# A new written order for all five engines from block 1 on in a fused attention and two-layer mixture kernel

## Chip, cores and metric

The kernel runs on one core of one Trainium2 chip. The metric is the device time of one execution in microseconds (us); the kernel before has three measured runs and one more that was profiled. All times below are of that profiled execution unless they are called a median.

## What is computed

Everything is float32, and the result has to have float32's accuracy.

```
out_up    = repeat4( softmax(scale * q_d k_d^T) v_d )      q_d, k_d, v_d: means over 4 positions
out_local = softmax(scale * q k^T where |i-j| < 4) v
x = heads_to_channels(out_up + out_local)                  q, k, v: 4 x 8 x 576 x 64 -> x: 2304 x 512
x = (sigmoid(x @ w_gate) * (x @ w_val)) @ w_out            512 -> 1536 -> 512
h = x @ w_in;  g = h * tanh(softplus(h));  out = g @ w_out2   512 -> 2048 -> 512
```

## The kernel before

**Tiling.** The four batches are four blocks of 576 tokens. A block has its attention and then the first layer; the second layer follows for all tokens at the end. Each wide product is split into a high and a low part and computed as three matmuls into one PSUM tile.

**The long products of a block.** `m1_half` (L1416 to L1418) multiplies a weight slice of the ring `R` with the tokens: 12 matmuls, 128x128 weights against 288 columns, into a tile `ps_m`. `m1` (L1442, L1443) makes the gate on ACT and DVE, and `fin` splits it into `G` (L425 on ACT, L426 on DVE). `m1out_part` (L1429, L1431, L1433) multiplies `G` with the output weights, 12 matmuls of the same shape into `ps_o`. `m1out` copies finished tiles to `stage` (L1473, L1476 on ACT), POOL makes differences of them (L1485), and `put` splits these (L1459 on ACT, L1460 on DVE) and parks them in DRAM (`x2d`, issued by SP at L1492 and L1498).

**Attention of the next block beside it.** While the long products of block b run, the attention of block b+1 runs in pieces between them. Its products are short ones. Two are full-height transposes or 72-row ones against an identity: L604 (loaded `tok` to `kT`, `qT`), L738 and L856. Four have operands of 64 rows or 64 columns: L699 (pooled scores), L753 (pooled values), L808 (local scores) and L896 (local values). The local softmax is L816 and L820 on DVE (mask and maximum, reading the PSUM tile of L808), L833 on ACT (exponential with row sums), L651, L652 and L844 on DVE (normalizing), L856 on PE, the copy L308 on ACT, L896 on PE and the join L915 on DVE. The copies out of L604 are L310 on ACT. Short products use a pool `at` of three PSUM banks, long products a pool `mm` of five.

**A stay** is from here on a run of short products on PE between two long ones.

**Loads and their queues.** SP issues the attention's loads (`tok` L552, `araw` L557, `vw` L572), the reload of the weights (`d<-wd`, L453, 512 KB each) and most stores. Weights that come in as 64-bit words are narrowed: POOL L390, then DVE L398, L399 and L403; the narrowed tiles are written to `wd` and read again. POOL issues the first loads of the second layer, `xu` (L1957, in `units2` and after it, 512 KB each).

**The second layer.** `product` (L2029 to L2031) is 12 matmuls of 256 columns, `m2out` (L2042 to L2044) is three of 512; `phase` puts them together. The first products follow two warm-up matmuls (L2013).

**What sets the order.** The steps of a block are traced in one way, which fixes the instructions and what each depends on. Then `written_order` rearranges every engine's instructions by a dictionary `RUNS`, one string for each of PE, ACT, DVE, POOL and SP. A word `step x n` moves the reading position by `step` and takes the next `n` instructions of the engine as traced:

```
step, _, n = word.partition("x")
at += int(step)
seq += own[at:at + int(n or 1)]
at += int(n or 1)
```

Each engine then has its instructions pinned in that order. It runs them one after another: where the next has to wait, all behind it on that engine wait too. The strings say nothing of times; each instruction starts when its operands are there.

Of the kernel before, what the change touches and what calls it, by code (L numbers as in the profile page):

```python
# [138 lines left out]
    'PE': '''0x1583 184x8 -192x12 204x4 -208x12 196x4 24x4 -228x24 204x4 -208x24 208x8 -216x16 12x12 -24x12 212x8  # L139
        24x2 2x2 2x2 -242x12 232x2 -234x24 198x2 -200x36 8x12 146x2 2x2 2x2 24x2 2x2 2x2 2x2 -194x12 8x24  # L140
        138x2 2x2 2x2 2x2 24 1 -2 -170x24 8x24 8x21 19x5 -24x3 83 -63x19 16x16 12x12 -24x8 16x36 8x24 -32x5
        1 29x12 -43 1 40x12 -28x4 24 1 1x12 -15 1 12x16 8x12 8x6 -14x4 -24 33 -34x7 16x4 24x8 -20x12 32
        -50x5 60 1 -2 1 -19x15 -40x12 80x2 2x2 2x2 -90x4 28x9 41x2 36x2 2x2 -40x2 4x2 -90x3 83x2 36x2 -36x2
        -52x8 -45x5 120x2 -82x4 -15x3 12x12 54x2 2x2 2x2 28x8 -34x2 -68x12 112x8 -64x12 -52x12 116x13 3x2
        2x2 -138x12 122x2 2x4 2x2 -17x3 10x2 2x2 -56x12 68x2 2x2 -106x12 96x2 -122x12 -32x12 52x12 68x2
        -12x2 -16x12 6x2 2x2 2x2 -40x12 28x24 36x4 -40x24 40x4 12x4 -14x2 2x2 -8x2 2x2 2x4 -56x12 72x2 2x2
        2x2 2x2 -12x2 36x2 2x2 2 -43x2 2x2 2x2 -72x12 86x2 2x2 1 2x2 -4x2 2x2 -80x24 -68x12 84x12 28x4
        -16x12 4x4 2x2 -64x2 64x2 -8x2 10x4 -12x2 2x4 -70x10 88x4 24x4 -56x12 44x4 24x4 -76x12 64x4 -64 87x4
        -91x11 80x4 24x4 -112x12 100x4 24x2 -122x12 110x2 -112x12 100x6 2x2 -4x2 2x2 24x2 2x2 -134x24 8x24
        80x2 2x2 -78x24 42x2 2x2 32 -31x2 -36x12 53x3 -30x2 -28x12 16x24 4x48 8 11x12 -23x11 -20x5 1 -2 1  # L150
        28x24 4x24 -56x4 24x2 26x12 -38 37x12 -49 48x4 4x12 -16x4 24x8 -20x12 32x13 3 1 -2 1 -7x3 -40x24
        68x4 2x2 2x2 -8x2 8x2 -8x2 -58x12 76x2 2x2 2x2 -38x2 38x2 -90x24 54x2 -56x12 46x2 2x2 2x2 24x4
        -68x24 44x4 24x8 -64x24 64x13 3x2 -5x3 2x4 2x2 2x2 -86x24 8x24 56x2 2x2 -30x24 -34x2 2x2 2x2 40x12
        -20x2 2x2 -12x2 2x2 20x12 -30x2 2x2 24x24 44x12 -56x24 60x12 -72x16 72x12 -84x4 12x6 2x2 -4x2 2x18
        80x12 -80x6 2x2 2x2 42x12 -28x2 -14x12 4x2 2x2 -8x2 2x2 4x2 -48x2 2x2 2x2 34x2 2x2 24x64 12x18 2x2 6
        11x12 -28x2 -8x2 2x2 2x2 -40x12 52x24 -47x11 36x600 36x12 -48x36 24x12 12x12 -24x12 -36x12 36x72
        24x24 -48x24 36x12 12x12 -24x12 -36x12 36x13 13x12 -24x12 -13 36x12 -24x12 48x12 -48x12 48x12 -60x12
        48x12 -36x12 -36x12 84x12 -48x24 27x2 -29x12 12x3 24x12 6x12 -52x13 3 -4x2 100x12 -110x2 15x3 135x12
        -132x3 -36x3 36x12 6x12 66x12 -78x3 42x12 -130 81x12 -39x3 -18x3 36x3 33x3 -96x3 150x12 6x12 -108x3
        132x12 -168x3 72x3 117x4 -217x3 33x3 90x2 61x12 -73 -78x3 160 -62x12 50x7 -72x3 -81x6 -9x3 36x6 30x3  # L160
        21x3 -24x3 78x12 -147x3 33x3 33x3 78x12 45x12 -51x12 66x12 -69x12 24x12 27x12 -189x3 21x3 -6x3 36x3
        132x12 -189x3 21x3 33x3 33x3 -60x3 -57x3 207x12 -132x3 21x3 -81x3 33x3 75x3 96x12 -75x3 -93x3 -6x3
        210x2 -176x3 33x2 61x12 65x9 -147 33x3 21x3 -84x3 117x12 38 -30x12 81x12 -222x3 33x3 -81x3 21x3 33x3
        30x3 21x3 -24x3 15x3 96x12 -30x12 102x12 -186x3 96x12 -75x3 96x12 9x12 -171x3 21x3 186x12 -30x12
        -186x3 33x3 -42x3 54x3 15x3 21x3 -78x3 33x3 33x3 -57x3 36x3 -6x3 33x3 21x3 33x3 33 5x12 6x12 -35x2
        -96x3 138x12 12x12 12x12 -165x3 33x3 21x3 -84x3 21x3 -24x3 33x3 18x3 12x3 18x6 12x3 105x12 -114x3
        21x3 51x12 -72x3 -24x3 126x12 -96x3 -24x3 24x3 15x3 81x12 -159x3 21x3 60x3 21x3 -72x2 25x3 -24x3
        21x3 21x3 -55 90x3 21x3 -69x3 93x12 -81x3 -57x3 114x3 15x3 -60x3 78x12 -147x3 21x3 21x3 21x3 54x3
        -54x3 -54x3 21x3 42x3 -24x3 3x12 21x3 15x3 15x3 -36x12 18x3 15x6 15x3 -6x3 -15x12 24x12 -66x12 24x15
        36x12 -48x3 18x12 -15x3 -6x3 33x12 3x12 6x12 33x12 -42x12 3x12 18x12 -123x3 27x3 15x3 75x12 -123x3  # L170
        27x3 111x12 -93x3 93x12 -78x2 -47x3 75x12 36x12 -108x3 27x2 -15 14 78x12 -78x3 12x3 15x3 48x12 -33x3
        -48x3 78x2 -5x2 -50x3 72x3 -21x12 9x9 -34 -4 -21x2 79x12 -90x3 57x12 -36x2 97x12 -30x12 -90x3 33x3
        -40 117x12 -57x3 33x3 21x3 -75x12 -39x3 -76 54x3 33x3 -72x3 150x12 -129x3 147x3 -96x3 -24x3 147x3
        -54x12 -108x3 111x12 -72x3 78x12 -114x3 117x12 -75x3 33x3 -93x3 171x12 -150x3 33x3 39x3 -96x3 33x3
        33x6 57x12 81x12 -126x12 159x12 -30x12 -168x3 75x12 -93x3 60x12 -51x3 33x3 75x12 -54x3 -81x3 21x3
        87x3 -96 62x12 -36x3 114x12 -93x3 -77x2 33x3 72x3 99x12 -30x12 -90x3 33x3 33x3 -132x3 111x12 -204x3
        33x3 33x3 21x3 54x3 33 56x12 -68x2 69x12 -30x3 30x12 15x3 -81x2 -95x3 204x3 -228x3 33x3 33x3 38
        -18x3 -45x3 33x3 84x12 60x12 -147x3 75x12 -60x3 90x3 -33x12 -15x3 57x12 3x12 -63x3 63x12 -132x3
        -18x3 147x12 -99x2 -5x3 9x3 -10 15x2 -8x3 9x3 -6x3 78x12 3x12 -109 33x3 -18x3 57x3 33x3 9x3 -36x3
        21x3 9x3 -84x3 57x3 9x3 -60x3 45x3 9x3 6x18 36x12 -48x2 46x2 -38x12 -22x3 19x5 -24x7 48x14 -45x7  # L180
        14x10 14x10''',
    'ACT': '''0x292 6 25 -28 -5 1 29 -18 20 -29 28 3 -31x2 -14 16 -7 -2 37 -2 -34x2 27 8 -30 -6 -17 16x2 3x2 -5 5
        -6 3 26 -24 5 -8 1 3 5 -8 4 5x2 -7 3 5 20 -64 52 22 -36 4 -4 -48 57 20 -29x4 27 -19 -41 -22 57x3 8
        -18 14 -12 6 9 -21 14 5 6 -17 5 -10 15 -9 -5 8 -4 7 7 -6 -2 7 -7x3 6 -5 1 -5 4 7x2 -8 10 -9x2 -4x2 9
        -4 8 -6 3 3 -12 -48 59 -2 -9 9x2 -18 17 -12 4 -5 15 -14 7 1 -2 2 5 2x2 -4 8 -43 27 2 25 -4 3 -29 29
        -9 -16x2 -5 4 15 3 -20 12 -13 1 7 -27 30 8 -5 6 -2 -2 -5 1 -20x2 16 5 -26 25 24 -67 41 -25 49 -11 1
        -42 39 2 -7 4 -5 5 10 -55 27 -28 42 -16 20 -6 -21 1 -5x2 22 3 3 -7 6 4 -2 -8 12 -2 -7 11 -5 -16 5 -2
        14 2 -13 6 -2 -6 13 -11 4x2 10 -24 38 -25 -2 9 -55 -7 53 2 11 -12 -55 73 -15x2 16 -4 -27 22 -70 65
        16 -35 4 12 -20 7 30 -33 3 37 -38 2 9x2 1 4 -84 95 -34 17 2 -19 12 -8 7 1 22 -19 -2 1 6 -93 90 2 12
        -21x2 8 -9x2 10 2 -2 -6 -98 62 30 20 -6x2 -4x2 -11 7 -3 6 -9 9 -2 2 9 3 -13 3 -6 2 6 4 -12 2 6 -7 -3  # L190
        12 3 -12 5 1 -10 4x2 12 -9 -2 20 -3 2 -9 -8 9 -8 4 -11 7 -3 -8 7 -10 2 19 -19 15 -5 -3 6 2 -69 62 -8
        10 5 -5x2 6 -3 -5 2 -3 6x2 11 -17 10 -7 8 -3 -11 10 1 3x2 -4x2 -13x2 27x2 -16 -14 -64 63x2 13 -3 2
        -3 3 2 -5 11 2 -14 3 -4 7 6 2 -9 14 -15 9 -18x2 8 -2 -12 14 10 -13 5 8 -12 11 -14 15 -13x2 13 -12 -2
        2x2 10 -9 11 6 -19 7 -6 10 -13 2 4 -5 2 11 2 -12 -2 3 11 -12 2 10 -13 2x2 -9 10 11 5 -11 -5 -4 1 2x2
        7 -17 11 -2 2x2 2 11x2 -6 -4 -7 4 -2 2 4 -2 -4 6x2 -14 13 -25 25x2 -11 7 13 -11 1 -4 12 -12 9 -8x2
        -3 2x4 5 1 -5 2 3 -7 4 -2 2x5 1 -2 11 -11 2 -3x2 9 -2 -8x2 19 -20 7 -8x2 8 -3 -7 18 -13 1 7 13 -21
        -2 1 -9 8 9 -4 -7 17 -12 3 1 -6 11 -7x2 20 -12 -25 10 3 21 -18 4 1 -7 6 -7 -20 27x2 -4 8 -13 6x2 16
        -43 20 12 -4 11 -9 -4x2 3 7 -8 -30 29 9 -14 24 -22 5 4 -38 32 5 10 -11 7 -8 -8 -22 28 -5 4x2 17 -8
        -40 34 4 -5 -8 18 -7 -13 18 -39 25 5x2 -4 -28 39 -10 9 -5 9 -5 -6x2 4x2 7 -2 -7 1x2 -8 -37 47 -36 35
        -6 5 -33 34 -2 -2 6 -32 26 -25 24x2 2 -3 5 -2 1x3 2 -25 22 -9 9 6 -17 14 -3 -4x2 2 2 -12 14 6 -17 5  # L200
        10 -8 -4x2 3x3 3 4 -2 -8 -5 7 10 -2 -5 -6x2 4x2 -4 10 -5 10 -15 14 -12 3 1 -6x2 9 -6 -3 7 9 -16x2 7
        -4x3 8 -8 17 -13 -6x3 7 -4 10 -16 4 10 -11 1 1x2 8 6 -16 -4 3 3 3 -4 9 -6 -5 4x2 3 -8 3 13 -8 -4 10
        -11 2 1 -5 4x2 -4 6 -4 7 -2 -4 5 -6 5 -6 5x2 -5''',
# [2073 lines left out]
```

## Time and profile before

| | us |
|---|---|
| median of three runs | 1012.32 |
| lowest, highest | 1008.45, 1016.48 |
| the profiled execution's own time | 1007.65 |
| its span in the profile | 1005.8 |

The span is what the profile's rows lie in, from 0 to 1005.8 us; 1.85 us of the execution's time lie around it. In the span, the attention of block 0 and what goes with it lasts to 185.7 us, the long products of the blocks to 613 us, and the second layer from there to the end. A matmul row's own duration includes its pipeline, so the distance from one start to the next is what it costs PE. The trace keeps two rows for one matmul of L808 and L896 and one row for a transpose and for a long matmul.

### The profile page before, as it was taken

How to read it: one execution, taken by the hardware profiler on the slowest of the kernel's cores; microseconds unless marked ns; L12 is line 12 of the kernel's file. 1: busy time of each engine (PE TensorE's matmuls, PEld its weight loads, DVE VectorE, ACT ScalarE, POOL GpSimd, SP SyncE). 2: the span in 40 equal slices, each digit the busy share in tenths (PEclk: the TensorE clock that was granted, in tenths of full speed). 3: DMA queues.
4: the chain of work that ended last, by engine and by line, in shares of the span. 5: the costliest groups of instructions: out<-in, count | busy, mean ns of one | idle time of the engine just before them, and what ended most of it. 6: DMA issues, size and time to landing. Idle time of an engine off the chain costs nothing.

```text
span 1005.8 us, 20645 instructions
## 1 busy us (share of the span) xinstructions
PE 977.7 (97%) x8113; PEld 911.0 (91%) x8113; DVE 673.9 (67%) x1097; ACT 560.9 (56%) x1259; POOL 251.8 (25%) x276
## 2 busy tenths in 40 slices
...
GB/s 225 156 235 185 186 253 262 238 137 163 178 118 180 214 92 165 102 151 116 234 199 126 87 170 228 331 192 252 183 249 265 282 231 240 124 147 140 154 56 105
DMA packets 160897, 184.86 MB, mean 184 GB/s; under 512 B 68512, under 2 KB 124064, under 8 KB 160288
## 3 DMA queue, kind: packets, MB, share of 16 engines
...
## 4 chain that ended last, share of the span: by engine, by line
PE 76%; DMA 10%; DVE 6%; ACT 3%; issue 2%; POOL 1%; SPq 1%; ACTq 0%; POOLq 0%; DVEq 0%
PE ps_m L1416 9%; PE ps_m L1417 9%; PE ps_m L1418 9%; PE po L2042 6%; PE po L2044 6%; PE po L2043 6%; PE h L2029 6%; PE h L2031 6%; PE h L2030 6%; PE ps_o L1429 3%; PE ps_o L1433 3%; PE ps_o L1431 3%; DMA tok<-in_q_dram 1%; DMA d<-wd 1%; DMA raw<-in_moe_w_out_dram 1%
## 5 line engine op out<-in xcount | busy, mean ns | idle before, releaser
L1416 PE MATMUL ps_m<-R 128*128 128x288 f32 (+2 forms) x768 | 232.4, 304 | 0.0
L1418 PE MATMUL ps_m<-R 128*128 128x288 f32 (+2 forms) x768 | 227.6, 296 | 0.0
L1417 PE MATMUL ps_m<-R 128*128 128x288 f32 (+2 forms) x768 | 227.6, 297 | 0.0
L2029 PE MATMUL h<-xu,R 128*128 128x256 f32 x512 | 145.0, 283 | 3.5 <-ACT hs L2175 2.1
L1416 PEld LDWEIGHTS ps_m<-R 128*128 128x128 f32 x768 | 144.6, 189 | 3.8 <-issue 1.3
L1418 PEld LDWEIGHTS ps_m<-R 128*128 128x128 f32 x768 | 144.9, 189 | 0.3 <-issue 0.2
L1417 PEld LDWEIGHTS ps_m<-R 128*128 128x128 f32 x768 | 144.9, 189 | 0.1
L2030 PE MATMUL h<-xu,R 128*128 128x256 f32 x512 | 144.4, 282 | 0.0
L2031 PE MATMUL h<-xu,R 128*128 128x256 f32 x512 | 144.0, 282 | 0.0
L1429 PE MATMUL ps_o<-G,R 128*128 128x288 f32 x384 | 115.3, 301 | 0.0
L2042 PE MATMUL po<-wo,g 128*128 128x512 f32 x288 | 113.0, 393 | 1.1 <-ACT o L2080 1.1
L1433 PE MATMUL ps_o<-G,R 128*128 128x288 f32 x384 | 113.3, 295 | 0.3 <-DVE R L426 0.3
L1431 PE MATMUL ps_o<-G,R 128*128 128x288 f32 x384 | 113.0, 294 | 0.0
L2043 PE MATMUL po<-wo,g 128*128 128x512 f32 x288 | 112.5, 391 | 0.0
L2044 PE MATMUL po<-wo,g 128*128 128x512 f32 x288 | 111.4, 392 | 0.0
L2029 PEld LDWEIGHTS h<-xu,R 128*128 128x128 f32 x512 | 97.1, 190 | 8.3 <-ACT hs L2175 2.7
L426 DVE TENSOR_TENSOR R<-d,R 128x512 fp32r<-128x512 f32 (+1 forms) x108 | 79.3, 744 | 33.2 <-ACT R L425 33.1
L2030 PEld LDWEIGHTS h<-xu,R 128*128 128x128 f32 x512 | 97.3, 190 | 3.4
L390 POOL TENSOR_SCALAR rebias<-raw 128x512 f32<-128x512 f32 x33 | 56.5, 1712 | 174.8 <-DVE d L403 73.3
L2031 PEld LDWEIGHTS h<-xu,R 128*128 128x128 f32 x512 | 97.1, 190 | 0.0
L425 ACT CAST R<-d 128x512 fp32r<-128x512 f32 (+1 forms) x108 | 67.3, 642 | 45.3 <-DMA d<-wd 23.5
L1429 PEld LDWEIGHTS ps_o<-G,R 128*128 128x128 f32 x384 | 71.9, 188 | 1.2
...
## 6 DMA issues: line engine op xcount, KB each, us to landing
d<-wd SPq DMA_DIRECT2D x54, 512.0 KB
xu<-x2d SPq DMA_DIRECT2D x45, 512.0 KB
raw<-in_moe_w_out_dram SPq DMA_DIRECT2D x28, 512.0 KB
wd<-d SPq DMA_DIRECT2D x18, 512.0 KB
raw<-in_moe_w_in_dram SPq DMA_DIRECT2D x16, 512.0 KB
wo<-wd SPq DMA_DIRECT2D x16, 512.0 KB
...
raw<-in_moe_w_gate_dram SPq DMA_DIRECT2D x12, 512.0 KB
```

The costliest lines, as they stand in the source:

```text
L1416: PE.matmul(p[:, 0:n], lhsT=wh, rhs=xh[:, c, ts], start=(c == 0), stop=False)
L1417: PE.matmul(p[:, 0:n], lhsT=wh, rhs=xl[:, c, ts], start=False, stop=False)
L1418: PE.matmul(p[:, 0:n], lhsT=wl, rhs=xh[:, c, ts], start=False, stop=(c == KD - 1))
L1429: PE.matmul(p[:, 0:SUB], lhsT=hi[:, o:o + 128], rhs=gt[:, f, 0, ts], start=(f == 0), stop=False)
L1431: PE.matmul(p[:, 0:SUB], lhsT=hi[:, o:o + 128], rhs=gt[:, f, 1, ts], start=False, stop=False)
L1433: PE.matmul(p[:, 0:SUB], lhsT=lo[:, o:o + 128], rhs=gt[:, f, 0, ts], start=False, stop=(f == KF1 - 1))
L2029: PE.matmul(o, lhsT=wh, rhs=x[:, c, 0, :], start=(start and k == 0 and c == 0), stop=False, skip_group_check=True)
L2030: PE.matmul(o, lhsT=wh, rhs=x[:, c, 1, :], start=False, stop=False, skip_group_check=True)
L2031: PE.matmul(o, lhsT=wl, rhs=x[:, c, 0, :], start=False, stop=(c == 1), skip_group_check=True)
L2042: PE.matmul(p, lhsT=gh, rhs=w[:, 0, :], start=(f == 0), stop=False)
L2043: PE.matmul(p, lhsT=gh, rhs=w[:, 1, :], start=False, stop=False)
L2044: PE.matmul(p, lhsT=gl, rhs=w[:, 0, :], start=False, stop=(f == 2 * NQ - 1))
```

## The change

Only the strings of `RUNS` change. All instructions, tiles, buffers and dependences are the same; each engine gets another permutation. The beginning of each string and its end are as before:

| engine | instructions | same at the beginning | same at the end |
|---|---|---|---|
| PE | 7169 | 1535 | 654 |
| ACT | 1074 | 283 | 65 |
| DVE | 1097 | 295 | 75 |
| POOL | 272 | 93 | 6 |
| SP | 570 | 132 | 39 |

On PE that is the trace from 185.7 to 888.7 us. The core of the diff (each string is some 20 to 40 lines):

```diff
 RUNS = {
-    'PE': '''0x1583 184x8 -192x12 204x4 -208x12 196x4 24x4 -228x24 204x4 -208x24 208x8 -216x16 12x12 -24x12 212x8
...
-    'POOL': '''0 1 1 -4 3 -3 2 1 1 1 1 1 -10 1 1 1 1 1x76 3 -4 15x2 -14 -4 16x4 -17 -4 3x5 3x2 -5x3 8 3 -3x2 -3
...
-    'SP': '''0x137 19x3 5 -20 20x2 16 -34 35 -16x2 2 9 -28 8 8 2 -29x2 1 13 -30 -2 23 -21 -7 22 78 -86 -17 52 -27
...
+    'PE': '''0x1535 12x12 -24x12 12x24 184x4 -188x24 164x4 -168x12 180x4 -184x12 172x4 -176x12 188x4 -192x28
...
+    'POOL': '''0 1 1 -4 3 -3 2 1 1 1 1 1 -10 1 1 1 1 1x77 2x2 -4x2 13x5 -16x2 14 -15x4 3x2 -5x2 9x2 -11 10x3 13
...
+    'SP': '''0x132 24 -25 24 -22 -2 -3 24 5 1 -33 16 7x2 11x2 2 -23 22 -26x2 -17 29 12 -3 -24 7 22 -44 21 8 -30
```

Read out, the two PE strings hold, between their common beginning and the first product of the second layer:

| stays of short products | before | after |
|---|---|---|
| stays with L808, L896, L753 or L699 in them | 54 | 20 |
| stays with transposes alone | 20 | 44 |
| unbroken runs of L808 | 43 | 26 |
| unbroken runs of L896 | 50 | 35 |
| unbroken runs of L753 | 8 | 4 |
| changes between L2029-type and L2042-type matmuls in the second layer | 56 | 48 |

In eight of the 20 stays of after, four PSUM tiles of the pool `at` (which has three banks) are filled in one stay; for example two tiles of L808, eight matmuls each, then two more in the same stay.

Four stretches, read out (the number in front is the place in the engine's own order; `tok` loads are numbered here from the first one of the stretch):

```
SP before   132 x2d<-sx, 133 x2d<-stage, 134 d<-wd, 135 x2d<-sx, 136 x2d<-stage,
            137 tok 1 (k), 138 tok 2 (q), 139 tok 3 (k), 140 tok 4 (q), 141 x2d<-G, 142 tok 5 (k)
SP after    132 tok 1, 133 x2d<-sx, 134 tok 2, 135 x2d<-stage, 136 x2d<-sx, 137 x2d<-stage,
            138 tok 3, 139 tok 4, 140 tok 5, 141 d<-wd
DVE before  364 L398 (d<-rebias), 365 L651, 366 L651, 367 L652, 368 L844 (first), ... 371 L844 (second)
DVE after   354 L651, 355 L652, 357 L844 (first), 361 L651, 363 L652, 364 L844 (second); that L398 behind them
POOL before 207 xu5, 208 xu1, 209 xu2, 210 L1485, 211 L1485, 212 xu6, 213 L1485, 214 xu7, 215 L1485, 216 L1485
POOL after  207 to 211 the five L1485, 212 xu6, 213 xu5, 214 xu7, 215 xu1, 216 xu2
SP, the loads of tok at the end of block 1:  places 165, 207, 209, 233 before; 169, 174, 178, 195 after
```

At the first of these places, PE before runs the two first groups of L604 one right behind the other; after, 24 long matmuls stand between them. At the end of block 1, the copy L310 of the first group stands on ACT behind six copies of `stage` and splits before, and ahead of most of them after; the L604 groups there are spread one at a time between pairs of `m1_half`. The second layer's products begin before with those of xu5 and xu1, then xu2; after with xu1, then xu2, then xu5 and xu6.

## Rows read from the trace of the kernel before

**Rows 1.** The page: busy time of the engines, and the chain that ended last.
```profile
PE 977.7 (97%) x8113; PEld 911.0 (91%) x8113; DVE 673.9 (67%) x1097; ACT 560.9 (56%) x1259; POOL 251.8 (25%) x276
...
PE 76%; DMA 10%; DVE 6%; ACT 3%; issue 2%; POOL 1%; SPq 1%; ACTq 0%; POOLq 0%; DVEq 0%
```

**Rows 2.** Windows by stage: length, then PE, PEld, DVE, ACT, POOL; clock, DMA, GB/s.
```profile
185.70:348.00 162.30, 156.09 (x1438) 146.47 (x1436) 89.08 (x188) 81.80 (x257) 40.15 (x46) 1.00 0.60 172
348.00:486.00 138.00, 134.19 (x1260) 125.84 (x1260) 79.60 (x179) 77.13 (x250) 25.82 (x24) 0.99 0.44 132
486.00:613.00 127.00, 125.27 (x957) 124.58 (x953) 76.37 (x142) 57.44 (x126) 42.51 (x55) 1.00 0.50 156
613.00:888.70 275.70, 271.16 (x1749) 246.15 (x1750) 202.21 (x224) 162.63 (x207) 59.08 (x54) 1.00 0.72 237
```

**Rows 3.** Timeline of PE, two stays with L896: start, duration, line, count.
```profile
287.82 0.29 PE L1417 MATMUL ps_m<-R 128*128 128x288 f32 x1
287.95 0.29 PE L1418 MATMUL ps_m<-R 128*128 128x288 f32 x1
288.18 0.57 PE L896 MATMUL ps_la<-ETl,vw 64*64 64x58 f32 x20
288.68 0.40 PE L1417 MATMUL ps_m<-R 128*128 128x288 f32 x1
288.92 0.30 PE L1418 MATMUL ps_m<-R 128*128 128x288 f32 x1
...
291.35 0.29 PE L1418 MATMUL ps_m<-R 128*128 128x288 f32 x1
291.57 0.33 PE L896 MATMUL ps_la<-ETl,vw 64*64 64x58 f32 x4
291.83 0.40 PE L1418 MATMUL ps_m<-R 128*128 128x288 f32 x1
292.06 0.29 PE L1416 MATMUL ps_m<-R 128*128 128x288 f32 x1
```

**Rows 4.** Timeline of PE, a stay with transposes alone.
```profile
297.48 0.29 PE L1433 MATMUL ps_o<-G,R 128*128 128x288 f32 x1
297.61 0.67 PE L738 MATMUL ps_gt<-ident,Eg 72*72 72x72 f32 x8
298.07 0.38 PE L1429 MATMUL ps_o<-G,R 128*128 128x288 f32 x1
298.29 0.30 PE L1431 MATMUL ps_o<-G,R 128*128 128x288 f32 x1
```

**Rows 5.** What PE waited for: us in total, times, longest.
```profile
PE ps_t L604 <- DMA tok<-in_k_dram: 3.3, 2, 2.4
PE ps_lt L856 <- DVE El L844: 3.2, 2, 2.8
...
PE ps_t L604 <- ACT kT L310: 1.8, 1, 1.8
...
PE ps_t L604 <- DMA tok<-in_q_dram: 1.4, 2, 0.9
```

**Rows 6.** Chain of waits, the load behind the first L604 stall.
```profile
188.33 7.35 DMA tok<-in_q_dram
```

**Rows 7.** Timeline of DVE, the instruction ahead of the late L844.
```profile
261.92 0.43 DVE L398 TENSOR_SCALAR d<-rebias 128x512 int32<-128x512 int32 x1 [3.21 <-DMA wd<-d]
```

**Rows 8.** Window over the first L604 stall, columns as in rows 2.
```profile
188.00:196.00 8.00, 5.06 (x39) 4.65 (x38) 1.49 (x3) 3.14 (x8) 0.00 (x0) 1.00 0.95 232
```

**Rows 9.** Groups by line, 185.7 to 613 us: the reader of L808's PSUM tile.
```profile
L816 DVE SCALAR_TENSOR_TENSOR El<-ps_l,mask 128x256 f32<-128x256 f32 x20 | 8.3, 420 | 13.5 <-PE ps_l L808 13.5
```

**Rows 10.** Timelines at the second layer's start: POOL's, then PE's.
```profile
605.91 0.74 POOL L1485 TENSOR_TENSOR stage<-stage 128x256 f32<-128x256 f32 x1 [5.03 <-DMA x2d<-stage]
...
617.00 0.39 PE L2029 MATMUL h<-xu,R 128*128 128x256 f32 x1 [0.43 <-ACT h L2166]
```

**Rows 11.** DMA view, 575 to 620 us: size and median us to landing.
```profile
xu<-x2d POOLq DMA_DIRECT2D x7, 512.0 KB, 6.1
```

More of the change, by code (lines that the diff above doesn't have):

```diff
@@ L138 @@
 RUNS = {
-    'PE': '''0x1583 184x8 -192x12 204x4 -208x12 196x4 24x4 -228x24 204x4 -208x24 208x8 -216x16 12x12 -24x12 212x8
[L140 to L203, printed above, removed]
@@ new lines @@
+    'ACT': '''0x283 1 12 -15 1 1x2 -3 4 -3 3 -4 1 2 5 23 3 -6 -21x2 24 -23 25 -26 -3 -6 -5 4 2 28 3 -30x2 32 -33
+        27 -28 1 1 1 -6 30 -30 -23 23 2x2 5 -2 35 -38 4 23 -24 -10 -28 40 30 -5x2 -30 25 -25 21 8 -28 -44 66
+        -24 -3 4 -14 20 20 -24 -3 10 -15 5 -5 28 -9 6 -20 -39 27 18 -11 18 -4 8 -83 70 -21 20 -14 23x2 -6 5
+        -12 11 3 -11 15 -8 -9 6 5x2 1 7 -19 3x3 16x2 -6 8 -15 14 -17 -2 4 12x2 -17 16 -17 5 -3 5x2 -7 3 12 4
+        -9 8 1x2 -15x2 -66 83 23 -10 2 -9x2 -28 36 -34 24 3 1 -4 -5 -27 36 -35 7 -6 2 30 -2 -30 23 -22 22
+        -22 25 -41 10 10 -52 69 -15 -13x3 50 -27 23 -6 -2 -3 -11 10 -42 37x2 4x2 -68 22x2 43 9 -5 -50 43 1
+        -23 29 -33x2 2 21 1 4 -28 30 4 -34 28 -3 -34 39 -15 -22 21 3 13 -14 -26 30 7 -3 4 -13 4 -2 10 6 -6
+        -7 7 -14 3 15 -14 31 -19 13 -28 3 -52 60x2 -9 -6 21 -19 16 -8 -8 29 -29 10 -6 25 -34 18 -4 3 -11 7 9
+        -2 3 8 2 -35 5 16 -25 29x2 9 -28 31 5 -38x3 -51 54 10 -94 93 5 -23 20 4 10 -30x2 26 -27x2 6 5 -104
+        118 3 2 -29 7 -3 26 -18 -7 8x2 3 -12 -3 11 2 -15 14 -14 16x2 5 -2 2 9 -8 -78 69 4x2 19 -14 -2 18 -9
+        -26 -6x2 30 -27 3 6x2 5 10 -9 -56 67 -26 26 -18x2 -4 5 -14 19 -15 22 3 1 -6 -4 -10 12 -11 -10 19 10
+        4 -26 1 10x3 -24 33 -5 4x2 -5 -9 12 -9 -17 17 20 -28 27 -28x2 -9 18 16 -94 76 18 -14 2 -9x2 12 -13x3
+        16 2 -9 3 10 -15 9 -19 9 2x2 1 11 -12 7 -5 -25 22 2 -23 25 10 3 -19 10 -4 -35 27 3x2 2 -2 2x2 3 -23
+        20 8 5 -12x2 -7 3 -42 44x2 3 -3 11 -12 7 -31 35 3 -17x2 3 -2 2x2 13 -13 4 -5 7 -6 3 -2 8 -7 8 -9 11
+        -9 8 -11 3 -2 4 3 -44 41 -23 -11 27 6 -2 6 7 -14x2 1 -2 -12 12 2x2 -3 7 -31 30 -7x4 5 -3 3 2 -5 -3 4
+        -2 2 1 -2 1x2 1 -2 11 -11 2 -3x2 9 -2 -8x3 18 -19x2 5 2 -9 5x2 9 -9 9 -10x2 19 -20x2 9 8 -13 -7 10
+        -22 16x2 4 6 -9 1x2 -15 34 -12 -5 -6 5 3 -4 4 10 -11 8 -9 -4 4x2 -3 20 -19 6 -38 39 -10 9 -4x2 3 5
+        -44 37x2 9 -14 8 -6 5 -38 51 -15 3 -4 13 -10 -40 49 -11x2 20 -25 -26 29x2 -3 12 -5 4 7 -20 12 -7x2
+        -8 18 -50 42x2 -4 -31 39 -7 8 -3 2 -42 42 3x2 4 -15 12 -9x2 -4 3 2x2 3 -49 48x2 2 -2 1 -42 4 36 -5
+        -25 35 -34 31 -5x2 -4 7 -8 2 4 3 -9 4 1 1 5x2 -7 -5 10 -7 9 -9x2 -3 -29 33 9x2 -11 2 1 5 -11 4x2 7 6
+        -15 -5 7 3 6 -11 4 -5 9 -6x2 7 6 -15 -5 18 -12x2 2 -3 3x2 4 -8 7 9 -16x2 7 -4x3 8 -8 17 -13 -6x3 7
+        -4 10 -16 4 10 -11 1 1x2 8 6 -16 -4 3 3 3 -4 9 -6 -5 4x2 3 -8 3 13 -8 -4 10 -11 2 1 -5 4x2 -4 6 -4 7
+        -2 -4 5 -6 5 -6 5x2 -5''',
```

121 lines of the change are left out of this document (82 added, 39 removed).

## Prediction

> **What bounds the kernel now.** I read the page first: PE is busy 97% of the span and makes 76% of the chain that ended last, DMA 10%, DVE 6% [rows 1]. Then the windows by stage: in each stage that the change touches PE is busy all but a few us, every other engine is under 75%, and the clock is full [rows 2]. So only two things can give time: what PE's own order costs PE, and the few waits left. Busy time hides the first, since a row's duration overlaps the next one's; I therefore read the timeline by starts. Two neighbouring long matmuls start 0.13 us apart (287.82 to 287.95) [rows 3]. The list of what PE waited for gives the second [rows 5].
>
> **Part 1: fewer stays with 64-row products.** From the last long matmul before a stay to the second one after it, 287.95 to 288.92 is 0.97 us with ten matmuls of L896 (twenty rows), 291.35 to 292.06 is 0.71 us with two [rows 3]. Without the change of kind two spacings of 0.13 would stand there, so the stays cost 0.71 and 0.45 us. The eight further matmuls cost 0.26 us, 0.033 each; so a stay of no matmul at all would cost 0.45 - 2 x 0.033 = 0.38 us. That is the fixed price: the way in takes 0.23 instead of 0.13, and the first long matmul after it is again followed late (288.68 to 288.92, 0.24). The same for transposes alone: 297.48 to 298.29 is 0.81, less 0.26 is 0.55; the eight take 0.46 us (297.61 to 298.07), and the fixed part is 0.09 us [rows 4]. The two orders have 54 and 20 stays of the first sort, 20 and 44 of the second: 34 x 0.38 = 12.9 us saved, 24 x 0.09 = 2.2 us added, **-10.7 us**. Other work hides nothing of this, as PE is what ends last. Bounds: if only the way in belongs to the kind (0.10 us), 34 x 0.10 = 3.4, less 2.2, is -1.2; if the added stays of transposes cost nothing, -12.9. I take -10.7, since both stays of [rows 3] show the late second start too. The 56 and 48 changes in the second layer I put at nothing: both sorts there use all 128 rows, as most transposes do, and by the price of a stay of transposes eight changes are 0.7 us at most.
>
> **Part 2: waits of PE that should go.** (a) At the beginning of block 1 two groups of L604 wait 2.4 us for the k tile and 0.5 us for the q tile (the other times in these two rows are at the end of block 1) [rows 5]; the q load took 7.35 us [rows 6] on DMA engines 0.95 busy, 232 GB/s [rows 8]. After, these loads stand ahead of four parks of `x2d` (144 KB each) and a reload of 512 KB; at 232 GB/s these bytes are 2.5 + 2.3 us, more than the 2.9 us waited, and the second group has 24 long matmuls (24 x 0.13 = 3.1 us) of cover besides. -2.9 us, bounds -2.9 and 0. The reload moved back serves weights first used some seven `m1_half` later (7 x 12 x 0.13 = 11 us), which hides it. (b) L856 waits 2.8 us for L844 [rows 5], because L398 ahead of it on DVE's queue waits 3.21 us for a DMA [rows 7]. After, L844 and its sums stand ahead of L398, and behind L398 only narrowing waits, which PE needs much later. -2.8 us, bounds -2.8 and 0. (c) At the end of block 1 PE waits 1.8 us for the copy `kT` and 0.9 and 0.9 us for loads [rows 5]. The copy and the loads both move forward, but they still have the same neighbours in ACT's and SP's queues, and the groups are needed one by one; I count half: -1.8 us, bounds -3.6 and 0. Together **-7.5 us**. What is late next there: the long products themselves, whose operands have no wait in [rows 5].
>
> **Part 3: what the new order adds.** Eight stays fill four PSUM tiles where the pool has three banks, so the fourth waits until DVE has read the first. The reader of L808's tile takes 0.42 us [rows 9], and PE stands until then with all long products queued behind: 8 x 0.42 = **+3.4 us**. It is 0 if the reader is done while the other two tiles are filled, and three times as much (+10.1) if two DVE instructions of that length stand ahead of it; no row of before shows four tiles in a stay, and I take the reader alone. At the start of the second layer POOL issues xu1 and xu2 last, behind the stage difference that ended at 605.91 + 0.74 = 606.65 us [rows 10]. With a landing of 6.1 us [rows 11] all at once would be there at 612.8, one strictly behind another five would be at 637.2; the second product of before began at 617.0 [rows 10]. So 0 to +20; the seven loads of [rows 11] overlapped, so I stay near the lower end: **+1 us**. For fresh waits anywhere in 700 us of new order I put a quarter of the 9.3 us of (a) to (c), **+2.3 us** (0 to +9.3).
>
> **A rule weighed against part 1.** The Trainium skill, TensorEngine Tiling (Array Packing), Key Properties, says that the array drains when the tiling mode changes, and not when only the tile does. [Rows 3] agree as far as they go: the changed kind costs 0.38 us a stay and the transposes 0.09. By that rule alone a stay would pay at its two changes, 0.10 us each by the starts of [rows 3] (the way in 0.23 and the way out 0.24 instead of 0.13), so 34 x 0.20 less 2.2 is -4.6 us instead of -10.7; the rest of the 0.38 us would be no drain, and is a saving only if it goes with the stay.
>
> **The sum.** -10.7 - 7.5 + 3.4 + 1 + 2.3 = -11.5 us. The profiled execution took 1007.65 us, so 996.1. The median of the three runs lies 4.7 us above that execution; with it the forecast is **1000.8 us**. A difference of about 1% (10 us) is what a measurement of this kernel can tell from none.
>
> **Rivals.** (1) The stays are saved but given back at the banks: each fourth tile waits for a busy DVE, +10.1 instead of +3.4, and fresh waits reach half of 9.3: 1007.65 - 10.7 - 7.5 + 10.1 + 1 + 4.7 for those waits + 4.7 to the median = 1009.9. For it: DVE is half busy in these stages [rows 2]. Against: most of its instructions are no longer than the reader. (2) The other side: the loads xu1 and xu2 arrive one behind another, +20, and PE stands before the second product of the second layer. 1000.8 - 1 + 20 = 1019.8. It decides the sign from the point where xu2 lands some 12.5 us later than the second product needs it. For it: five loads now stand behind a chain of five differences, each waiting for DMA (5.03 us at the last one [rows 10]). Against: DMA engines are half idle there [rows 2], and the whole chain moves forward with PE. (3) The change doesn't do what it says for the transfers: bytes only change places. The engines are 0.95 busy over the first stall [rows 8], so what moves ahead pushes something back that is needed next; (a) and (c) gain nothing, 1000.8 + 2.9 + 1.8 = 1005.5. The Trainium skill, DMA: Bandwidth & Descriptors, Issuing engines are not separate DMA queues, speaks for this: transfers of all issuing engines interleave on the same 16 engines. (4) The changes of kind are cheap: the fixed 0.38 us is mostly something that the longer stays keep, and part 1 is -1.2: 1000.8 + 9.5 = 1010.3. For it: the price comes from short stays; against, both stays give it.
>
> **How the numbers follow.** Forecast 0.60, with a range of its own from 991 to 1005; rival 1 0.15, rival 2 0.06, rival 3 0.09, rival 4 0.10. The low end of the whole range: all of part 2 (-9.3), -12.9 in part 1 and no price in part 3 give 1007.65 - 22.2 + 4.7 = 990, and 988 leaves room for waits that I have not named. The high end takes in rivals 1, 3 and 4 at 1011 and leaves out rival 2. Faster by over 1% means under 1002.2: nine tenths of the forecast's 0.60 and a little of rival 3, 0.57. Slower by over 1% is rival 2, 0.06. Within 1%: 0.37.
>
> **What would show it.** Right: PE's busy windows up to 613 us shorter by some 15 us in all with the same matmuls; stays of L808 and L896 in bunches, each still with 0.23 us in and 0.24 us out; no wait of L604 for `tok` over 1 us at the start of block 1, none of L856 for L844; new waits of L808 or L896 for DVE, eight or so, under half a us each. Wrong: waits for DVE's readers of over 1 us in the bunched stays (rival 1), a wait of L2029 for `xu` (rival 2), the same wait for `tok` at another place (rival 3), or a bunched stay that takes as long as its parts did (rival 4).

## The result and the profile after

The change made the kernel faster: 983.34 us, median of four runs (982.2 to 984.82), against 1010.61 us before (four runs), ratio 0.9722 with a 95% interval of [0.9675, 0.9769]. The profiled execution took 982.2 us with a span of 980.4. The forecast was 1000.8 and its range ended at 988: the direction was right, the size was less than half of what came.

The page of the kernel after, busy time and chain that ended last. Its lines are numbered two higher than before (L606 is L604 of before, L810 is L808, and so on).

```profile
PE 962.6 (98%) x8113; PEld 906.2 (92%) x8113; DVE 675.9 (69%) x1097; ACT 558.8 (57%) x1259; POOL 252.0 (26%) x276
...
PE 88%; DVE 6%; DMA 3%; issue 1%; ACT 1%; POOL 1%; SPq 0%; POOLq 0%; DVEq 0%
```

Against [rows 1], DMA's share of the chain fell from 10% to 3%, and PE's rose from 76% to 88%. The windows by stage say where the time went: first three of after, then the same block stretch of before (columns as in [rows 2]).

```profile
187.20:586.80 399.60, 398.53 (x3650) 390.35 (x3649) 250.76 (x509) 214.09 (x629) 109.55 (x125) 1.00 0.56 164
586.80:863.30 276.50, 272.57 (x1750) 247.54 (x1749) 199.16 (x224) 162.04 (x208) 57.50 (x54) 0.99 0.74 241
863.30:980.40 117.10, 113.08 (x656) 99.67 (x654) 71.15 (x75) 53.26 (x63) 0.00 (x0) 1.00 0.32 104
```

```profile
185.70:613.00 427.30, 415.56 (x3651) 396.89 (x3649) 245.04 (x508) 216.38 (x632) 108.48 (x125) 1.00 0.52 154
```

All of it came from the block stretch, from the first rearranged long product to the first warm-up matmul of the second layer: 427.2 us before, 399.6 after. There PE is now idle for 1.1 us in 400. The second layer's stretch went from 275.7 to 276.5, block 0 before it from 185.7 to 187.2, and the common end stayed 117.1.

PE's waits from 183 to 620 us, beside [rows 5]; the whole list of after for that stretch:

```profile
PE h L2031 <- ACT h L2168: 1.9, 1, 1.9
PE ps_m L1420 <- DVE R L428: 0.4, 1, 0.4
PE ps_l L810 <- DVE xn L917: 0.3, 1, 0.3
```

None of the waits of [rows 5] is left; the one of 1.9 us belongs to the second layer. To part the gain I read every start-to-start distance of PE in the stretch. The usual distance of each kind of neighbours (by the kinds of the two matmuls and of the one before them) is the median over both kernels; their sum is the spacing, and what is left over is the rest. The rest holds the waits, time at a lower granted clock, and, with a minus, distances shorter than the usual one, as where the tiles of a long stay overlap; so it can be below 0.

| kernel (the edits are told below) | stays: 64-row, transposes | block stretch | spacing | rest |
|---|---|---|---|---|
| before | 54, 20 | 427.2 | 413.5 | 13.7 |
| after | 20, 44 | 399.6 | 401.3 | -1.6 |
| after, run again | 20, 44 | 399.6 | 401.3 | -1.6 |
| before, joined stays | 32, 20 | 418.4 | 406.5 | 11.9 |
| before, three moves | 54, 20 | 420.8 | 413.5 | 7.3 |
| before, both | 32, 20 | 418.8 | 406.5 | 12.4 |
| before, three moves and spread L604 | 54, 22 | 417.5 | 413.5 | 3.9 |
| before, all of these | 31, 22 | 415.2 | 406.1 | 9.1 |
| after, 34 splits | 54, 44 | 414.7 | 412.9 | 1.8 |
| after, 17 splits | 37, 44 | 405.8 | 406.9 | -1.1 |
| after, L604 packed | 20, 41 | 401.5 | 401.3 | 0.3 |
| after, SP's stretch of before | 20, 44 | 401.1 | 401.3 | -0.2 |
| after, two moves on ACT | 20, 44 | 399.6 | 401.3 | -1.7 |
| after, transposes joined | 20, 27 | 399.9 | 401.1 | -1.2 |

So the 27.6 us are 12.2 of spacing and 15.3 of rest. The line between the two depends on the grouping: with other groupings of the same rows (kinds by line, the two rows of a 64-row matmul as one) the spacing falls by 11 to 16 us. The stretch of the kernel after came out the same to a tenth in two executions, while whole times moved with block 0; the verdicts below therefore rest on the stretch, and whole times stand beside them. Every other stretch is that of one execution, and experiments 6, 7, 9 and 11 were run once.

The rest is not waits alone. In the kernel before the granted clock is 0.51 over the 3.5 us behind the waits at the end of block 1 (PE was busy for 8.37 of the 11.90 us ahead), and the long matmuls there stand 0.24 us apart instead of 0.13. Two windows (columns as in [rows 2]) and two rows of PE's timeline:

```profile
346.00:357.90 11.90, 8.37 (x65) 7.59 (x64) 4.01 (x8) 7.75 (x19) 2.73 (x5) 1.00 0.79 187
357.90:361.40 3.50, 3.50 (x20) 3.10 (x19) 0.69 (x2) 1.20 (x4) 3.42 (x3) 0.51 0.02 8
```

```profile
358.25 0.44 PE L1416 MATMUL ps_m<-R 128*128 128x288 f32 x1
358.49 0.44 PE L1417 MATMUL ps_m<-R 128*128 128x288 f32 x1
```

That is the lower of TensorE's two levels, 1.2 GHz, and costs about 1.4 us there. The stretch has the same for 3.4 us in experiments 1 (from 264.6 us), 2 (204.0) and 12 (270.4) and for 6.8 us in experiment 3 (263.4), each time within 1 us of the end of a wait of PE, and costs some 1.5 us for each 3.4. In both executions of the kernel after, in every edit of it and in experiment 9 the stretch has none. The waits of 2.4 and 2.8 us at 192 and 260 us in the kernel before were not followed by it, so a wait alone doesn't decide it.

### The profile page after: what moved, and what is told of

Same layout as the page of the kernel before. It is cut to its first block, busy times and chain, and to the rows that moved or that the text cites. A ratio compares the mean times of both kernels' runs of the same rounds, so it can differ in the third digit from the quotient of the medians.

```text
span 980.4 us, 20632 instructions
## 1 busy us (share of the span) xinstructions
PE 962.6 (98%) x8113; PEld 906.2 (92%) x8113; DVE 675.9 (69%) x1097; ACT 558.8 (57%) x1259; POOL 252.0 (26%) x276
## 4 chain that ended last, share of the span: by engine, by line
PE 88%; DVE 6%; DMA 3%; issue 1%; ACT 1%; POOL 1%; SPq 0%; POOLq 0%; DVEq 0%
PE ps_m L1418 9%; PE ps_m L1420 9%; PE ps_m L1419 9%; PE po L2044 6%; PE po L2046 6%; PE h L2031 6%; PE po L2045 6%; PE h L2033 6%; PE h L2032 6%; PE ps_o L1431 5%; PE ps_o L1435 5%; PE ps_o L1433 5%; DMA R<-wi2d 1%; PE ps_t L1000 1%; PE ps_t L606 1%; PE ps_la L898 1%
## 5 line engine op out<-in xcount | busy, mean ns | idle before, releaser
L428 DVE TENSOR_TENSOR R<-d,R 128x512 fp32r<-128x512 f32 (+1 forms) x108 | 83.2, 783 | 28.9 <-ACT R L427 28.7
```

## The experiments

Whole strings were not exchanged one engine at a time, nor (b) and (c) undone in the kernel after, so what each engine's new order gives by itself is not shown. Smaller edits were made instead. Diffs are given in read-out form.

**1. Joined stays in the kernel before (PE alone).**

```diff
 PE, 22 times
-  stay A, 2 to 14 long matmuls, stay B
+  stay A, stay B, the same long matmuls      (or the long matmuls first)
```

> The kernel before, PE's string alone changed: where two stays with 64-row products stood up to 14 long matmuls apart, they are joined; 32 such stays instead of 54, transposes' stays 20 as before, all other engines' orders as before. Theory (a stay costs PE 0.38 us whatever stands in it): 22 x 0.38 = 8.4 us less, ratio 0.992, and the waits for the k tile, for L844 and for the copy kT stay where they are. Rival (stays are cheap, the change gained by its waits alone): within 2 us of the kernel before. Second rival (joined stays wait for the banks): no gain, and new waits of L808 or L896 for DVE of 0.4 us each.

Measured: ratio 0.9951 [0.992, 0.9981]; stretch 427.2 to 418.4, spacing -7.0, which is 7.0 / 22 = 0.32 us a stay. The price per stay holds; "cheap" falls. The rest fell only from 13.7 to 11.9, but its waits did not stay where they were, as had been expected: that for L844 fell from 2.8 to 1.2 us, and two new ones came (lines five lower than before; L1428 is a long matmul, L694 is L699).

```profile
PE ps_o L1428 <- DVE R L421: 1.6, 1, 1.6
PE ps_g L694 <- ACT Eg L707: 1.4, 1, 1.4
...
PE ps_lt L851 <- DVE El L839: 1.2, 1, 1.2
```

**2. Three moves in the kernel before (SP, DVE, ACT).**

```diff
 SP
-  x2d, x2d, d<-wd, x2d, x2d, tok 1, tok 2, tok 3, tok 4, x2d<-G, tok 5
+  tok 1, x2d, tok 2, x2d, x2d, x2d, tok 3, tok 4, tok 5, d<-wd, x2d<-G
 DVE
-  L398, L651, L651, L652, L844, ..., L652, L844
+  L651, L651, L652, L844, ..., L652, L844, L398
 ACT
-  L1473, L425, L425, L1473, L1473, L1473, L1476, L310, L310, L310
+  L310, L310, L310, L1473, L425, L425, L1473, L1473, L1473, L1476
```

> The kernel before, PE's string as it was: on SP the five tok loads of the start of block 1 ahead of the weight reload and woven between the parks as in the new order, on DVE the one L398 behind the two L844, on ACT the first three copies L310 of the next block ahead of the stage copy they stood behind. Theory (each wait is made by one place in one queue): -2.9 at 192 us, -2.8 at 260 us, -1.8 to -3.6 at 348 to 357 us, together -7.5 to -9.3 us, ratio 0.991 to 0.993. Rival (transfers only change places): the wait at 192 us stays or turns up in the next L604, -3 us or less in all.

Measured: the whole time shows nothing (ratio 1.0013 [0.9973, 1.0053]), the stretch fell by 6.4 us, all of it rest, and less than the 7.5 to 9.3 expected. The places differ. Two rows of this kernel's list of what PE waited for (its lines are five lower than before: L599 is L604, L851 is L856, L839 is L844):

```profile
PE ps_t L599 <- DMA tok<-in_q_dram: 2.5, 1, 2.5
...
PE ps_lt L851 <- DVE El L839: 0.9, 1, 0.9
```

The 2.5 us are not at 192 us any more but at 201 us, before a later group of L604: there the loads only changed places, as the rival said. At 260 us the wait fell from 2.8 to 0.9 us, and DVE's timeline shows what is late next: the sums now wait for ACT's exponentials, the 2.15 us in brackets.

```profile
261.41 0.17 DVE L646 TENSOR_REDUCE sum<-pairs 128x8 f32<-128x16 f32 x1 [2.15 <-ACT El L828]
261.50 0.19 DVE L647 RECIPROCAL sum<-sum 128x8 f32<-128x8 f32 x1
261.73 0.69 DVE L839 TENSOR_TENSOR El<-El,sum 128x512 f32<-128x512 f32 x1
```

At the end of block 1 the moved copies took the excess from 3.8 to 1.3 us: one copy moved on ACT also brought the loads forward that had waited for its buffers.

**3. Both edits together in the kernel before.** The diffs of 1 and 2.

> The edits of the two other kernels together (PE's joined stays, and the three moves on SP, DVE and ACT). Theory: the two terms add, -8.4 and -7.5 to -9.3, so -16 to -18 us, ratio 0.982 to 0.984. Rival (one hides the other, PE waiting as long as its queue got shorter): not better than the better of the two alone.

Measured: ratio 0.9983 [0.9946, 1.0021]; the stretch is 418.8, no better than the joined stays alone. The spacing was saved (406.5), and the rest went back from 7.3 to 12.4. Its waits on PE (lines ten lower than before, L689 is L699):

```profile
PE ps_g L689 <- ACT Eg L702: 2.6, 1, 2.6
PE ps_t L594 <- ACT R L415: 1.8, 1, 1.8
PE ps_t L594 <- DMA tok<-in_q_dram: 1.6, 1, 1.6
PE ps_t L594 <- DMA tok<-in_k_dram: 1.1, 1, 1.1
```

A PE that comes sooner meets other operands not ready, with ACT as the one late. Of the 5.1 us by which the rest is longer than in experiment 2, some 1.5 are the longer time at 1.2 GHz (6.8 us against 3.4). The two terms don't add while the other engines keep their old orders.

**4. 34 splits in the kernel after (PE alone).**

```diff
 PE, 34 times in the 20 stays
-  short products of tile A, short products of tile B, 3 long matmuls
+  short products of tile A, 3 long matmuls, short products of tile B
```

> The kernel after, PE's string alone changed: in its bunched stays, 34 times three long matmuls are put between two tiles' short products, so 54 stays with 64-row products instead of 20, the transposes' 44 as they are. Theory (0.38 us a stay): 34 x 0.38 = 12.9 us more than the kernel after, some 996 us; less up to 1.3 us of waits for banks that the long matmuls now cover. Rival (stays are cheap): within 2 us of the kernel after, some 984 us.

Measured: the stretch went from 399.6 to 414.7, +15.1, of which +11.6 is spacing, 0.34 us a stay, and +3.5 rest (the whole 15.1 laid on the stays would be 0.44 us each). The timeline of PE in this kernel shows two such pieces (L808 is on its old line here):

```profile
231.66 0.29 PE L1418 MATMUL ps_m<-R 128*128 128x288 f32 x1
231.88 1.27 PE L808 MATMUL ps_l<-kT,qT 64*64 64x64 f32 x48
233.09 0.40 PE L1416 MATMUL ps_m<-R 128*128 128x288 f32 x1
233.32 0.30 PE L1417 MATMUL ps_m<-R 128*128 128x288 f32 x1
233.46 0.29 PE L1418 MATMUL ps_m<-R 128*128 128x288 f32 x1
233.68 0.68 PE L808 MATMUL ps_l<-kT,qT 64*64 64x64 f32 x16
234.29 0.40 PE L1416 MATMUL ps_m<-R 128*128 128x288 f32 x1
```

Each piece pays the way in again (233.46 to 233.68, 0.22 for 0.13) and the late second start (233.09 to 233.32, 0.23 for 0.13). Its median was 1003.38 us, ratio 0.9955 [0.992, 0.999] to the kernel before: without bunched stays over half of the stretch's gain is lost. The median is 20 us above that of the kernel after, not 15, but in the profiled execution block 0 alone was 7.5 us longer: the granted clock of its first 184 us was 0.94, against 0.98 there.

**5. The kernel after, run again beside 6 to 8.** 

> The kernel after unchanged, as the measure for the kernels beside it and for the spread of its runs. Both theories: 982 to 986 us.

Measured: 984.03 us, ratio 0.9787 [0.973, 0.9844].

**6 and 7. The first L604 groups packed again on PE, and SP's places of before, each alone in the kernel after.**

```diff
 PE (6)
-  group 1, 24 long, group 2, 12 long, group 3, 12 long, group 4, 12 long, group 5, ...
+  groups 1 and 2, 12 long, group 3, 12 long, groups 4 and 5, ...
 SP (7)
-  tok 1, x2d, tok 2, x2d, x2d, x2d, tok 3, tok 4, tok 5, d<-wd
+  x2d, x2d, d<-wd, x2d, x2d, tok 1, tok 2, tok 3, tok 4, tok 5
```

> The kernel after, PE's string alone changed: the first eight groups of L604 of block 1 packed as in the kernel before (two, one, two, one, two groups in a stay instead of one each). Theory (PE's spread of the groups is what gives the loads time, since the same loads moved forward alone only moved the wait from 192 to 201 us): waits of L604 for tok of 2 to 3 us come back between 193 and 210 us. Rival (SP's new order is enough by itself): no wait over 0.5 us there.

> The kernel after, SP's string alone changed: places 132 to 141 as in the kernel before (four parks and the 512 KB reload ahead of the tok loads), PE with its spread groups. Theory (the first group of L604 stands at the same place in both orders and has no cover but the earlier load): a wait of 2 to 2.9 us at 193 us, and none at the later groups. Rival (the bytes share the DMA engines, their order is no matter): no wait over 0.5 us.

Measured: +1.9 us in the stretch with packed groups, by one wait at 199 us, but for the copy out of the banks and not for `tok` as had been expected (first row; lines two lower than before, L602 is L604). With SP's old places +1.5 us, by one wait for `tok` at 195 us, shorter than the 2 to 2.9 expected (second row, of the other kernel; lines one higher, L605 is L604). So both the earlier issue and the spread carry a part of what (a) gave, and the spread also gives ACT time to empty the banks.

```profile
PE ps_t L602 <- ACT qT L308: 1.6, 1, 1.6
```

```profile
PE ps_t L605 <- DMA tok<-in_k_dram: 1.3, 1, 1.3
```

**8. Two moves on ACT in the kernel after.**

```diff
 ACT, start of the second layer
-  L1459, L1459, L1459, L2166
+  L1459, L2166, L1459, L1459
 ACT, near 776 us
-  L425 (waits for POOL), L2151, L2080, L2080
+  L2151, L2080, L2080, L425
```

> The kernel after, two moves on ACT alone: at the start of the second layer the copy that the second product waits for goes ahead of two casts that wait for POOL's stage differences; near 776 us the two copies of po and one of hs go ahead of a cast that waits for POOL. Theory (each remaining wait of PE is made by one place in one queue): the 1.9 us wait at 589 us falls to some 0.7, the 1.2 us wait at 776 us falls or goes: -1.2 to -2.4 us against the kernel after. Rival (the wait is only uncovered elsewhere, as with the moves made in the kernel before): within 0.5 us of it.

Measured: 983.7 us against 984.03 beside it, nothing. The 1.9 us wait fell to 0.7 as expected, and new ones for transfers took its place (what PE waited for in this kernel, on the lines of before):

```profile
PE h L2029 <- DMA xu<-x2d: 2.7, 2, 1.8
PE h L2029 <- DMA R<-wi2d: 2.7, 1, 2.7
PE h L2029 <- ACT h L2166: 0.7, 1, 0.7
```

In the second layer the loads are next in line, so these moves on one queue were worth nothing there.

**9. Three moves and spread groups in the kernel before.**

```diff
 PE, beside the diffs of 2
-  groups 1 and 2, 12 long, group 3, 12 long, groups 4 and 5, 24 long, group 6, ...
+  group 1, 12 long, group 2, 12 long, group 3, 12 long, group 4, 12 long, group 5, ...
```

> The kernel before with the three moves on SP, DVE and ACT of the run that made those alone, and on PE the first eight groups of L604 of block 1 spread one to a stay, 12 long matmuls apart (two, one, two, one, two groups in a stay before). Theory (the loads need both, the earlier issue and the spread groups): the wait of 2.7 us at 201 us falls under 1 us and the stretch from 185 us to the first product of the second layer is some 2 us shorter than without the spread (420.8 us). Rival (the wait is made by the loads' bytes ahead of it on the DMA engines): it stays at 2 us or more wherever the group stands.

Measured: the stretch is 417.5, 3.3 us shorter than without the spread, and what is left at these groups is 0.6 us at 204 us, where it was 2.7 at 201. Some 1.5 of the 3.3 us are the 3.4 us at 1.2 GHz behind that wait, which this execution doesn't have. For these loads it takes both: the loads moved ahead on SP and a PE that doesn't ask for two groups at once.

**10. 17 splits in the kernel after.** The diff of 4, 17 times.

> The kernel after, PE's string alone changed: 17 of the 34 splits, so 37 stays with 64-row products instead of 20. Theory (a price per stay): half of what 34 splits cost in the block stretch (15.1 us with waits, 11.6 us by spacing), so +5.8 us by spacing and 0 to 2 us of waits. Rival (the price came from the waits that splitting made): under 3 us.

Measured: 992.26 us, ratio 0.9853 [0.9771, 0.9934]; stretch +6.1, spacing +5.6, which is 0.33 us a stay (0.36 with the rest). The price is per stay.

**11. Joined stays of transposes in the kernel after.**

```diff
 PE, 17 times
-  4 transposes, 1 to 24 long matmuls, 4 transposes
+  8 transposes, the same long matmuls      (or the long matmuls first)
```

> The kernel after, PE's string alone changed: 17 stays of transposes alone are joined to a neighbour of the same sort (27 instead of 44), the 20 stays with 64-row products as they are. Theory (0.09 us for a stay of transposes): 1.5 us less spacing in the block stretch, unless waits for tok, banks or copies come back, 0 to 3 us. Rival (a stay of transposes costs as much as one with 64-row products): 6 us less.

Measured: spacing -0.2 us, so 0.01 us a stay, and 0.4 us of rest more. A stay of transposes costs next to nothing beyond its own matmuls.

**12. All edits of 1, 2 and 9 in the kernel before.** No further diff.

> The kernel before with all that was done to it singly: the three moves on SP, DVE and ACT, the spread groups of L604 at the start of block 1, and joined stays (31 with 64-row products instead of 54). If the two terms are independent: 23 x 0.32 = 7.4 us of spacing and the 9.8 us that moves and spread gave, so the stretch from 185 us to the first product of the second layer falls from 427.2 to 410 us. Rival (a PE that runs ahead meets the old orders of ACT and DVE sooner, as when joined stays and moves were first put together): waits of 2 us and more come back at L699, L856 or L604, and the stretch is 413 to 418 us.

Measured: ratio 0.9916 [0.9886, 0.9945], stretch 415.2: the rival, though with no wait as long as its 2 us. The spacing fell by 7.4, the rest is 9.1 instead of 3.9. PE's waits in this kernel (L689 is L699, L594 is L604):

```profile
PE ps_g L689 <- ACT Eg L702: 1.8, 1, 1.8
PE h L2003 <- ACT stage L1463: 1.4, 1, 1.4
PE ps_t L594 <- DMA tok<-in_q_dram: 1.4, 1, 1.4
PE ps_t L594 <- ACT kT L300: 0.8, 1, 0.8
PE ps_g L689 <- ACT ETl L298: 0.8, 1, 0.8
```

Bunching 23 stays by hand together with every move I had named brings 12 us of the 27.6. What is missing is 4.8 of spacing (11 more stays bunched, not tried here) and 10.7 of rest that no edit tried took away, some 1.4 of it the 3.4 us at 1.2 GHz. It goes in the kernel after, and which places of its joint order carry it stays open.

## Why the prediction was wrong in size

**Part 1 was right.** -10.7 forecast, -12.2 measured as spacing. The price of a 64-row stay was 0.38 by two stays of [rows 3] and is 12.2 / 34 = 0.36 over all, 0.32 to 0.34 in the three edits that changed only their number; with all of the stretch laid on the stays these give 8.8 / 22 = 0.40, 15.1 / 34 = 0.44 and 6.1 / 17 = 0.36. The 2.2 us for added stays of transposes, from one stay of [rows 4], are next to nothing (experiment 11). Rival 4 has fallen; so has the weaker price (-4.6) that I worked out beside the Trainium skill's rule that a change of the tiling mode drains TensorE (TensorEngine Tiling (Array Packing), Key Properties). The runs agree that the change of kind costs, but that price was 0.20 us a stay, and the edits gave 0.32 at least.

**Part 2 is the step that failed.** In its sum the three places in [rows 5] are all the waits that the old order had, and one of them counts half: -7.5 us. With the 3.4 and 2.3 us that part 3 charged in the stretch, the forecast for the rest was -1.8 us; it measured -15.3. Of the waits it named, (a) gave 3.3, (b) 3.0 and (c) 3.8 us, as distances over the usual, 10.1 together. I counted all of (a) and (b) but only half of (c), because "they still have the same neighbours". The neighbours changed: ACT makes the first copy at once, and PE waits nowhere. Two rows of after for (b) and (c), of DVE and of ACT, and between them the PE row that no longer waits:

```profile
247.49 0.69 DVE L846 TENSOR_TENSOR El<-El,sum 128x512 f32<-128x512 f32 x1
```

```profile
249.87 0.60 PE L858 MATMUL ps_lt<-ident,El 128*128 128x128 f32 x4
```

```profile
334.25 0.60 ACT L312 ACTIVATE kT<-ps_t 128x512 f32<-128x512 f32 x1 [1.39 <-PE ps_t L606]
```

L846 ends 1.7 us before L858 starts; in before it came 2.8 us too late. The copy L312 waits for PE, not PE for it. Beside these, five smaller waits of before went that I had not named, 3.2 us together, the largest 1.55 us before the second layer's first warm-up. It was in the list of before, next to those of [rows 5]:

```profile
PE h L2013 <- ACT stage L1473: 1.4, 1, 1.4
```

Another 4.2 us lie in many distances that differ by less than 0.15 us each. Over 1 us of them are the matmuls at 1.2 GHz behind the waits of (c); whether the other part belongs to the stays or to the order of the other engines is not shown.

**Part 3 charged too much, but its mechanism held.** It charged +6.7 us: +3.4 for eight fourth tiles, +1 at the second layer's start, +2.3 for fresh waits "a quarter of the 9.3". The runs give about 2.3, 0.8 and 0.7. The fourth tile does wait for the reader, as one stay of after shows on PE (the single row is the start of the fourth tile) and on DVE:

```profile
224.00 0.29 PE L1420 MATMUL ps_m<-R 128*128 128x288 f32 x1
224.22 1.89 PE L810 MATMUL ps_l<-kT,qT 64*64 64x64 f32 x64
226.04 0.40 PE L1418 MATMUL ps_m<-R 128*128 128x288 f32 x1
226.28 0.29 PE L1419 MATMUL ps_m<-R 128*128 128x288 f32 x1
```

```profile
225.43 0.27 PE L810 MATMUL ps_l<-kT,qT 64*64 64x64 f32 x2
```

```profile
224.95 0.42 DVE L818 SCALAR_TENSOR_TENSOR El<-ps_l,mask 128x256 f32<-128x256 f32 x1 [1.38 <-PE ps_l L810]
225.54 0.42 DVE L818 SCALAR_TENSOR_TENSOR El<-ps_l,mask 128x256 f32<-128x256 f32 x1 [0.17 <-PE ps_l L810]
```

DVE, idle until then, has read the first tile at 224.95 + 0.42 = 225.37, and the fourth begins at 225.43. In experiment 4 a stay with one tile takes 0.61 us up to the long matmul behind it (233.68 to 234.29) and one with three 1.21 (231.88 to 233.09), so a further tile costs 0.30. Here the fourth brings it to 1.82 (224.22 to 226.04), 0.61 more: 0.31 us is the wait. In the three other stays with four tiles of L810 the fourth begins just as close behind its reader, at 293.21, 354.60 and 434.83. Three more of the eight have a distance of 0.47, 0.32 and 0.32 us over the usual, each ending 0.10 to 0.15 us behind an L917 of DVE. So seven of the eight wait, some 2.3 us together, of which the distances over the usual show 1.3. The list of PE's waits shows 0.3 of it, since the duration of a matmul's row reaches over a short gap. I had written that the price is 0 "if the reader is done while the other two tiles are filled". It can't be here: the reader starts 0.73 us after the first tile does and ends at 1.15, and at 0.30 us a tile the fourth would be due at 0.9. That the reader's 0.42 us lies near the 0.31 is therefore in part luck.

The fresh waits over 0.15 us are 0.5 and 0.2 us, both of long matmuls. The second layer's start: no wait for `xu` came. POOL issues all five loads in one piece, 11.3 us before the first product, and the differences that I put ahead of them are done by then:

```profile
572.38 0.91 POOL L1487 TENSOR_TENSOR stage<-stage 128x256 f32<-128x256 f32 x1 [2.22 <-DMA x2d<-stage]
576.25 3.90 POOL L1959 DMA_DIRECT2D xu<-x2d  x5 [2.96 <-DVE R L428]
581.53 0.73 POOL L1487 TENSOR_TENSOR stage<-stage 128x256 f32<-128x256 f32 x1 [1.38 <-ACT stage L1475]
```

In its place the second product waits 1.9 us for ACT's copy, and from 592.6 to 596.0 us the granted clock is 0.50; with the rest of the layer its stretch is 0.8 us longer. So rival 2 has no ground, and rival 1, which put 10.1 us on the fourth tiles, neither.

**The rivals.** Rival 3, that bytes only change places, was seen in the kernel before when the loads were moved and PE's order kept (experiment 2), and not in the kernel after. The Trainium skill's rule that I set beside it, that transfers of all issuing engines interleave on the same 16 engines (DMA: Bandwidth & Descriptors, Issuing engines are not separate DMA queues), is no reason against the change. The loads and the parks here are all issued by SP, and experiment 7 shows that their order on it counts, 1.5 us at 195 us; experiment 9 shows that it counts together with when PE asks. Of the signs that the prediction named, the bunches, the missing waits for `tok` and for L844 and the waits for DVE under half a us came; none of a rival's did.

**The range.** Its low end counted all of part 2 and no price in part 3 and came to 990; what lay under it were waits and distances that were each too small to be named, 3.2 + 4.2 us. Another 3.6 us of the miss are no mechanism: the sum added 4.7 us from the profiled execution to the median, and in the kernel after the median lies 1.1 us above it.
